# Attention and two MoE blocks on one core: a bound on x from v's sums of squares, new planned durations, filled TensorE gaps, and an order planned anew

## The chip, the cores and the metric

The kernel runs on one core of a Trainium2 chip. The metric is the device time of one execution in microseconds; lower is better. The core has a matrix engine (TensorE, PE in the profile, with its weight loads as PEld), a vector engine (VectorE, DVE), an activation engine (ScalarE, ACT), a general engine (GpSimd, POOL), and a sequencer that issues DMA transfers (SyncE, SP). Each engine works through its own queue in order; they wait for each other by semaphores.

## What is computed

```python
def rmsnorm(x, g):
    rms = np.sqrt(np.mean(x * x, axis=-1, keepdims=True) + 1e-06)
    return x / rms * g
# attention: q, k, v of 4 batches x 12 heads x 448 rows x 64
q_n, k_n = (rmsnorm(q, g_q), rmsnorm(k, g_k))
scores = np.matmul(q_n, k_n.transpose(0, 1, 3, 2)) / np.sqrt(64)
attn = softmax(scores)                       # max taken off, exp, divided by the sum
x = np.matmul(attn, v)                       # -> 1792 tokens x 768
# first block, w_in 768 x 2048, w_out 2048 x 768
h = x @ w_in;  g = h * sigmoid(1.702 * h);  x = g @ w_out
# second block, same sizes
h = x @ w_in2; g = h * np.clip(h + 3, 0, 6) / 6;  out = g @ w_out2
```

Inputs are float64 for the weights (read as 64-bit words and decoded on the chip) and float32 else.

## The kernel before

**Numbers as pairs of halves.** Every float32 operand of a large product is scaled by a power of two and split in two float16 parts, high and low; a product is three float16 matmuls (high x high, low x high, high x low). The scales come from sums of squares: a matmul with a matrix of ones adds them up over the partitions (`total`, L445), and DVE takes the square root's exponent (`root_exponent`, L460 and L463). The high part is a scaled copy on ACT, POOL or DVE (`scaled`: L480, L486, L483), the low part a subtraction on DVE (L495) or, in another form, on POOL or DVE (L510, L511).

**Stages.** For each of the four batches: load q, k and v (L969, L923); norm them (squares L972 or L985, sums L975, k times the gains L978, root L1004 to L1019, times the root L1029, high parts L1035, low parts L1047 and L1050); transpose by DMA; scores on PE (L1204, L1207), maxima on DVE (L1212), exponentials on ACT (L1217); the product with v (batch 0 in fp32: transposes on PE L1266 and products L1132; other batches in halves, L1165); x as halves (L1298 high on ACT, L1303 low on DVE); in-projection on PE (L1411) with a gate on ACT (L1456) and a product on DVE (L1460); out-projection on PE (L1479). The weights of the first block are decoded meanwhile, piece by piece (L618 or L623 the sign, L629, L604 to L614, L635). The attention of batch b + 1 runs beside the projections of batch b. The second block comes last (L1655 and L1770 on PE), by a scheme with fewer products whose operands are sums and differences of blocks (L716, L730).

**The bound on x.** After x's high part is made, `xsquare` (L1309) squares it on ACT and sums it; when all six head pairs are there, DVE takes the largest sum (L1375), a `total` matmul spreads it, and `root_exponent` gives `xe`. `x_scale` (L1390 on) multiplies it into the scale of the gated values. v has its own sums of squares `vm` (L926, once per head pair, on ACT), their largest is taken (L933), and `ev`, `sv`, `xf` are made of it.

**The order** is not written by hand. The program is first recorded as operations with dependencies (`Plan.op`), each with one or more engines that can do it (`ways`) and a planned duration (`t_pe`, `t_act`, `t_dve`, `t_fast` and so on). `Plan.order` then plays the program through with these durations: at each step it takes the operation that can start first, within a look-ahead, by a rank; where several engines can do an operation it picks the one that ends first with a bias per engine added. `Shared` durations are made longer where POOL and DVE work at the same time (`beside`). `LAG` is the planned time from one engine's end to another's start. The numbers in `CFG` shift ranks and biases; `own` shifts single operations by their place in the program. `keep_busy` puts matmuls without use (`fill`, L1960, 512 columns) into PE's queue where the plan sees a gap longer than `late` + `idle` and a PSUM bank is free:

```python
t1 -= CFG['late'] + CFG['idle']
if t1 <= t0 or not t0:
    return
...
n, i = int((t1 - t0) / 215.0) + 1, min(free)[1]
```

`late` (789) stays; `idle` is 1000 before. On the chip only the semaphores hold an engine: a planned gap is no wait by itself.

Of the kernel before, what the change touches and what calls it, by code (L numbers as in the profile page):

```python
# [9 lines left out]
F16 = mybir.dt.float16  # L10
# [24 lines left out]
    bias=[2580, 340, 2500, 1380, 5660],  # L35
    pw=[847, 1827, 3991690324, 32301064499],
    pn=[78, 1413, 6578, 11344],
    ps=[1104, 851, 1934, 2727],
# [4 lines left out]
    look=[0, 130, 60, 920, 540],  # L43
    off=[-9158, 408922, -29895, 22854, 24586, 19810, -27690, 67476, -181023, 15083, 120686, -34408, -37087, -37194, -689989, -31399, -23083, -347804, 11747, 208998],
    abias=44617,
    cuts=[],
    bias0=[2000, 440, 370, 120, 3040],
    bias1=[8820, 1540, 3900, 3250, 4520],
    dlook=2054,
    warm=9,  # L50
    late=789,
    idle=1000,
    pu=419,
    pmost=5,
    pv=1315,
    early_k=[0, 0, 0, 0],
    beside=0.9,
    own={
# [17 lines left out]
    [0.0, 0.0, 0.0, 0.0, 0.0],  # L76
# [3 lines left out]
def t_pe(n):  # L80
    return 0.445 * n
# [26 lines left out]
def t_dve_bits(n):  # L108
    return Shared(1.04 * n + 150)
# [6 lines left out]
def t_pool2(n):  # L116
    return Shared(1.5 * n + 380)
# [213 lines left out]
def attention_moe_moe_kernel(ctx, tc, q, k, v, g_q, g_k, w_in1, w_out1, w_in2, w_out2, out):  # L331
# [71 lines left out]
    bot_t, bot_ring = row(p_m, 19712, 1, [128, S], F16)  # L403
# [35 lines left out]
    def total(m, n, deps, slack=0.0):  # L439

        lease = Lease(mm_ring)
        t = lambda: mm_t[lease.slot][:, :n]

        def emit():
            nc.tensor.matmul(t(), lhsT=one.to_broadcast([128, 128]), rhs=m, start=True, stop=True)  # L445

        o = op((PE, 420, emit), deps, takes=lease)
        o.slack = slack
        return o, t, lease
# [112 lines left out]
    class Weight:  # L562
# [22 lines left out]
        def decoded(self, src, raw, cl):  # L585
# [60 lines left out]
            if self.wide:  # L646
                x = op([(POOL, t_pool(n), sign), (DVE, t_fast(n), sign_dve)], [o], takes=cl)
                x = op((DVE, t_fast(n), decode_a), [x])
                o = op([(POOL, t_pool(n), rebias_pool), (ACT, t_act(n), rebias_act), (DVE, t_fast(n), rebias_dve)], [x])
# [5 lines left out]
        def add(self, i, m, after):  # L655
# [3 lines left out]
            for j in range(i, i + m):  # L659
# [9 lines left out]
                squares.append(op((ACT, t_act(n, 1) + 45, square), [o] + after))  # L669
# [13 lines left out]
            o = op((DVE, 480 if self.inward else 550, scale), [o], gives=wl)  # L683
# [53 lines left out]
    class Units:  # L737
# [8 lines left out]
        def add(self, q, after, free):  # L746
# [7 lines left out]
            for j in range(2):  # L754
# [55 lines left out]
                if self.wide:  # L810
                    x = op([(POOL, t_pool(n), sign), (DVE, t_fast(n), sign_dve)], [o] + ends[:1], takes=None if j else lease)
                    x = op((DVE, t_fast(n), decode_a), [x])
                    o = op([(POOL, t_pool(n), rebias_pool), (ACT, t_act(n), rebias_act), (DVE, t_fast(n), rebias_dve)], [x])
# [4 lines left out]
                squares.append(op((ACT, t_act(n, 1) + 45, square), [o], gives=raw))  # L818
# [82 lines left out]
    class Batch:  # L901


        def __init__(self, b):
# [7 lines left out]
            self.xm, self.xe, self.t1 = small(NP), small(), small()  # L912
            self.c1, self.kg, self.x2m, self.x2e = small(KF), small(KF), small(KD), small()

    def add_values(bt, after):
# [16 lines left out]
        def largest():  # L932
            nc.vector.tensor_reduce(out=m, in_=bt.vm, axis=AX.X, op=ALU.max)  # L933
# [10 lines left out]
    def add_norm(bt, after):  # L944
# [136 lines left out]
        for grp in groups:  # L1081
# [3 lines left out]
                (DVE, 2300, lambda n=grp[0], m=m: root(n, m)), sum((p[1] for p in parts), [])  # L1085
# [84 lines left out]
    def add_units(bt, exp_after, arena_after, x_after):  # L1170
        b = bt.b
        bt.xlow, bt.pvs, xmax = [], [], []
# [6 lines left out]
        for n in range(NP):  # L1179
# [9 lines left out]
            ready = [None, None]  # L1189
            for grp in groups:  # L1190
# [45 lines left out]
                o = op((DVE, t_dve(m * S) + 60, maxes), [o])  # L1236
# [6 lines left out]
                o = op((DVE, 140, inv_z), es)  # L1243
# [15 lines left out]
                else:  # L1259
                    for i, tile_ in enumerate(grp):  # L1260
# [12 lines left out]
                        x = op((PE, 875, flip), [x], takes=tl, gives=dl)  # L1273
# [5 lines left out]
                for h, tiles_ in ((0, range(4)), (1, range(3, 7))):  # L1279
                    if ready[h] is None and all(turns[i] is not None for i in tiles_):  # L1280
                        pieces = [(128 * j, 0, 128, slots[4 * h + j]) for j in range(3)]
                        pieces.append((384, 64 * h, 64, slots[3]))
                        deps = [turns[i] for i in tiles_]
                        ready[h] = (join(pieces), deps) if b else add_head0(bt, n, h, pieces, deps)

            bl = Lease(bot_ring)
            bot = lambda bl=bl: bot_t[bl.slot]
# [29 lines left out]
            if b:  # L1317
# [12 lines left out]
                o = op((PE, 12 * t_pe(S) + 700, both_heads), deps[0] + deps[1] + vdone, takes=ml, gives=vl)  # L1330
# [3 lines left out]
                sq = op((ACT, t_act(S, 1), xsquare), [h], takes=bl, gives=bl)  # L1334
                xmax.append(sq)
                if early:
# [10 lines left out]
                    early.left = 2  # L1347
# [660 lines left out]
```

## Time and profile before

| | us |
|---|---|
| median of 3 runs | 1143.24 |
| lowest and highest | 1141.17, 1145.11 |
| the profiled execution | 1143.13 |
| its span, first to last instruction | 1141.3 |
| PE busy in the span | 1066.2 |
| DVE, ACT, POOL busy | 820.3, 721.0, 366.7 |

The profile names each instruction by engine, line, operation and tiles. Matmuls overlap in the array, so a busy PE is not a PE at its peak; the granted clock stands beside. A wait is put down to the instruction whose semaphore came last.

### The profile page before, as it was taken

The numbers are of one execution on the slowest core, as the hardware profiler recorded it, in microseconds if no ns is written. First come the engines' busy times: TensorE is split into PE (matmuls) and PEld (weight loads), VectorE is DVE, ScalarE is ACT, GpSimd is POOL, SyncE is SP. The second block draws the span as 40 slices with busy tenths as digits, with TensorE's granted clock in tenths as the row PEclk, the third lists the DMA queues.
The fourth block names the chain that finished last, engine by engine and source line by source line (L and its number), as shares of the span: only waits on it lengthen the run. The fifth ranks groups of instructions, "written<-read, shape, count | busy, mean of one in ns | idle before, by whom it ended". The sixth has DMA issues, their size and how long they took to land. (4 is left out here: it accounts for less than half of the span.)

```text
span 1141.3 us, 18028 instructions
## 1 busy us (share of the span) xinstructions
PE 1066.2 (93%) x6571; PEld 588.8 (52%) x6571; DVE 820.3 (72%) x1445; ACT 721.0 (63%) x1503; POOL 366.7 (32%) x337
## 2 busy tenths in 40 slices
PE   3888955999999999989999999999999999999998
PEld 1666522554554555545545555555555555555555
DVE  7998889988699764797765877694577456935342
ACT  5999868999868996578885646474565133512210
POOL 6764565443156101350001346452122103200000
PEclk9999985999999999999999999999999999999999
DMA  8876578999886997579895427733451151123034
GB/s 253 184 201 187 182 214 195 210 185 226 241 221 189 173 180 155 173 201 163 170 192 139 138 66 235 262 107 134 142 194 56 56 170 53 59 68 102 1 90 104
DMA packets 236712, 178.88 MB, mean 157 GB/s; under 512 B 194896, under 2 KB 220496, under 8 KB 235088
## 3 DMA queue, kind: packets, MB, share of 16 engines
q1 hardware_dynamic: 236624, 177.74, 59.6%
q8 instruction: 51, 0.84, 0.3%
q14 instruction: 37, 0.30, 0.1%
HBM read 97.88 MB, written 34.41 MB: 116 GB/s over the span
## 5 line engine op out<-in xcount | busy, mean ns | idle before, releaser
L1411 PE MATMUL mm<-xt,wa 128*128 128x448 f16 x1152 | 229.3, 357 | 6.0 <-DVE st L1460 5.9
L1479 PE MATMUL mm<-gt,wb 128*128 128x448 f16 x1152 | 228.2, 354 | 0.7 <-DVE wb L495 0.5
L1655 PE MATMUL mm<-wa,xt 128*128 128x448 f16 x972 | 189.0, 352 | 0.9 <-ACT wb L1677 0.9
L1770 PEld LDWEIGHTS <-gt 128*128 128x128 f16 x1344 | 131.5, 98 | 90.6 <-issue 2.7
L1411 PEld LDWEIGHTS <-wa 128*128 128x128 f16 x1152 | 113.9, 100 | 113.7 <-issue 14.2
L1479 PEld LDWEIGHTS <-wb 128*128 128x128 f16 x1152 | 112.3, 99 | 105.0 <-issue 3.1
L1655 PEld LDWEIGHTS <-xt 128*128 128x128 f16 x1008 | 98.5, 98 | 91.2 <-issue 1.4
L1217 ACT ACTIVATE p<-s,smalls 128x448 f32<-128x448 f32 x168 | 120.7, 720 | 7.1 <-DVE p L495 3.0
L1770 PE MATMUL s<-gt 128*128 128x384 f16 x576 | 99.3, 326 | 0.0
L1770 PE MATMUL s<-p,gt 128*128 128x384 f16 x516 | 96.2, 326 | 1.1 <-DVE wb L1809 0.5
L1212 DVE TENSOR_REDUCE smalls<-s 128x2 f32<-128x896 f32 (+1 forms) x96 | 91.5, 964 | 4.8 <-PE s L1207 4.7
L495 DVE SCALAR_TENSOR_TENSOR p<-p,smalls 128x448 f16<-128x448 f32 x108 | 78.1, 752 | 21.5 <-ACT p L480 21.2
L1204 PE MATMUL s<-gt 128*128 128x448 f16 (+1 forms) x192 | 62.6, 372 | 31.1 <-ACT p L1217 29.2
L1809 DVE SCALAR_TENSOR_TENSOR wb<-s,smalls,wb 128x384 f32<-128x384 f32 x69 | 39.7, 611 | 70.8 <-PE s L1770 70.7
L480 ACT ACTIVATE p<-p,smalls 128x448 f16<-128x448 f32 (+2 forms) x120 | 75.9, 667 | 11.1 <-DMA xt<-p 7.5
L1207 PE MATMUL s<-gt 128*128 128x448 f16 (+1 forms) x192 | 62.4, 368 | 0.0
L495 DVE SCALAR_TENSOR_TENSOR gt<-st,smalls,gt 128x448 f16<-128x448 f32 x64 | 52.5, 830 | 6.1 <-ACT gt L480 4.9
L1677 ACT ACTIVATE wb<-mm 128x448 f32<-128x448 f32 x21 | 11.3, 540 | 66.2 <-PE mm L1655 66.2
L480 ACT ACTIVATE gt<-st,smalls 128x448 f16<-128x448 f32 x49 | 32.1, 661 | 29.5 <-DVE st L1460 26.3
L1266 PE MATMUL mm<-gt,p 128*128 128x128 f32 x336 | 44.2, 280 | 6.2 <-DVE xt L1277 1.9
L510 POOL TENSOR_TENSOR p<-p 128x448 f16<-128x448 f32 x17 | 20.1, 1184 | 86.8 <-ACT p L480 70.9
L1165 PE MATMUL mm<-xt,gt 128*64 128x64 f16 (+3 forms) x858 | 47.3, 256 | 0.5 <-DMA xt<-p 0.4
(213 smaller groups left out, 1796.2 us busy)
## 6 DMA issues: line engine op xcount, KB each, us to landing
wr<-in_moe_w_in_dram SPq DMA_DIRECT2D x32, 768.0 KB, 4.9
wa<-park_x SPq DMA_DIRECT2D x21, 672.0 KB, 4.1
wr<-in_moe_w_out_dram SPq DMA_DIRECT2D x12, 1024.0 KB, 6.1
wr<-in_moe_w_out_dram SPq DMA_DIRECT2D x16, 768.0 KB, 4.6
qkd<-xt SPq DMA_DIRECT2D x18, 672.0 KB, 4.8
p<-in_v_dram SPq DMA_DIRECT2D x42, 224.0 KB, 4.1
x2d<-st SPq DMA_DIRECT2D x24, 224.0 KB, 3.0
park_x<-wa SPq DMA_DIRECT2D x2, 2688.0 KB, 13.2
```

Of the source, the lines that this page charges most:

```text
L480: nc.scalar.activation(out=dst(), in_=src(), func=AF.Copy, scale=s)
L495: nc.vector.scalar_tensor_tensor(out=dst(), in0=src(), scalar=s, in1=high(), op0=ALU.mult, op1=ALU.subtract)
L1165: nc.tensor.matmul(mm_t[ml.slot][64 * h:64 * h + 64, c:c + m * w], lhsT=vhl[:, 2 * (i % 4) + i // 4, part], rhs=pt[:, s:s + w, i, q0:q0 + ...
L1204: nc.tensor.matmul(o, lhsT=x[:, 64 * t:64 * t + m], rhs=x[:, 448:896], start=True, stop=False)
L1207: nc.tensor.matmul(o, lhsT=x[:, 64 * t:64 * t + m], rhs=x[:, 896:1344], start=False, stop=True)
L1212: nc.vector.tensor_reduce(out=nb, in_=s_t[sl.slot][:, :m, :S], axis=AX.X, op=ALU.max)
L1217: nc.scalar.activation(out=p(i), in_=s_t[sl.slot][:, i, :S], func=AF.Exp, bias=nb[:, i:i + 1], scale=alpha, accum_out=z[:, i:i + 1],)
L1266: nc.tensor.matmul(mm_t[tl.slot][:, 128 * j:128 * j + 128], lhsT=p(i)[:, c:c + 128], rhs=diag(), start=True, stop=True,)
L1411: nc.tensor.matmul(mm_t[ml.slot][:, :n], lhsT=w.inw(we, kc, f), rhs=x[:, xe, kc, :n], start=(kc == k0 and i == 0), stop=(kc == k1 - 1 and ...
L1479: nc.tensor.matmul(mm_t[ml.slot][:, :S], lhsT=W2.outw(we, fc, d * 128, 128), rhs=gv[:, ge_, fc, :], start=(fc == g.part.start and i == 0), ...
L1655: nc.tensor.matmul(self.bank(k), lhsT=w[:, we, fa, kc], rhs=xs[:, fb, xe, kc], start=first and kc == 0 and j == 0, stop=kc == 2 and j == 2 ...
L1770: nc.tensor.matmul(mm_t[banks[h].slot][:, :half], lhsT=g[:, ge, f, tb * 128:tb * 128 + 128], rhs=w4_t[part % 2][:, f, we, h * half:h * hal ...
```

## The change

1. *The bound on x.* `xsquare`, its buffer, the largest, the `total` matmul and the root for x are taken out. v's sums are now added over the six head pairs instead of their largest being taken, and x is bounded by that: the scale of the gated values uses `ev` and a constant.
2. *Planned durations* of most operations are set anew, `beside` goes from 0.9 to 1.15, and the planned time from a DMA's end to every engine from 0 to 300 ns.
3. *Fills.* `idle` goes from 1000 to 0.
4. *Order.* All of `CFG` that steers the planner is new, `own` entirely.

The diff, cut to its core:

```diff
-    idle=1000,
+    idle=0,
-    beside=0.9,
+    beside=1.15,
     own={
-        1: 18285, 2: 13033, 4: 14353, 7: 16590, 17: 60615, 21: 15124, 23: 56483, 26: 34835, 28: 63794, 29: 27563,
...
+        176: 15568.0, 200: 14590.0, 201: 2188290.0, 414: -9016.0, 418: 4574.0, 607: 1737030.0, 661: 1734682.0,
...
-    [0.0, 0.0, 0.0, 0.0, 0.0],
+    [300.0, 300.0, 300.0, 300.0, 300.0],
...
 def t_pe(n):
-    return 0.445 * n
+    return 0.4225 * n
 def t_fast(n):
-    return Shared(0.72 * n + 80)
+    return Shared(0.57 * n + 75)
 def t_dve_two(n):
-    return Shared(1.04 * n + 150)
+    return Shared(1.04 * n + 80)
 def t_dve_rest(n):
-    return Shared(1.04 * n + 205)
+    return Shared(1.04 * n + 135)
 def t_pool2(n):
-    return Shared(1.5 * n + 380)
+    return Shared(1.5 * n + 260)
...
-        (ACT, t_act(S, 3) + 200 * (i == 0) + 160 * (i == m - 1), lambda i=i, f=exps: f(i)),
+        (ACT, t_act(S, 3) - 35 + 325 * (i == 0) + 235 * (i == m - 1), lambda i=i, f=exps: f(i)),
...
         def largest():
-            nc.vector.tensor_reduce(out=m, in_=bt.vm, axis=AX.X, op=ALU.max)
+            nc.vector.tensor_reduce(out=m, in_=bt.vm, axis=AX.X, op=ALU.add)
...
-            def xsquare(n=n, high=high, bot=bot):
-                nc.scalar.activation(
-                    out=bot(), in_=high(), func=AF.Square, scale=2.0 ** -7, accum_out=bt.xm[:, n:n + 1]
-                )
...
-                sq = op((ACT, t_act(S, 1), xsquare), [h], takes=bl, gives=bl)
-                xmax.append(sq)
...
-        o = op((DVE, 200, largest), xmax + [bt.vscale])
-        o, whole, wl = total(m, 1, [o], 200.0)
-        xe = op((DVE, 330, lambda: root_exponent(bt.xe, whole())), [o], gives=wl)
...
-                times(g.t, emax, bt.ev, 2.0 ** -17)
+                times(g.t, emax, bt.ev, 2.0 ** -11)
...
-                times(g.t, g.t, bt.xe, 1.0)
...
-            bt.xscale.append(op((DVE, 870, x_scale), [xe, x]))
+            bt.xscale.append(op((DVE, 870, x_scale), [x]))
```

**What moves in the queues.** In all, fills go from 36 to 174; POOL's products, subtractions and scalings from 319 to 170, and most of what POOL loses stands on DVE. The two places shown next lie behind batch 0's last fp32 product. In the changed file the lines are: fill L1942, in-projection L1393, `total` L448, root times L1032 (L1029 before), gains L981 (L978), low parts L1050 and L1053 (L1047, L1050), low part by subtraction L513 on POOL and L514 on DVE (L510, L511), scaled copies L489 on POOL (L486).

PE's queue behind the last fp32 product of batch 0, before: three fills, then the in-projection (tiles wa and xt), 54 matmuls of it in a row behind the `total`:

```order
L1960 LDWEIGHTS ident_70
L1960 MATMUL mm_73<-ident_70 128x512
L1411 LDWEIGHTS wa
L1411 MATMUL mm_71<-xt,wa 128x448
L1411 LDWEIGHTS wa
L1411 MATMUL mm_71<-xt,wa 128x448
L1411 LDWEIGHTS wa
L1411 MATMUL mm_71<-xt,wa 128x448
L445 MATMUL mm_73<-smalls 128x1
L1411 LDWEIGHTS wa
L1411 MATMUL mm_72<-xt,wa 128x448
```

The same place now: eight fills, 21 matmuls of the in-projection, and then this; the pair of the last two rows of it stands 82 times, ahead of the in-projection's next matmul:

```order
L1393 LDWEIGHTS wa
L1393 MATMUL mm_71<-xt,wa 128x448
L1942 LDWEIGHTS ident_70
L1942 MATMUL mm_73<-ident_70 128x512
L1942 LDWEIGHTS ident_70
L1942 MATMUL mm_73<-ident_70 128x512
...
L448 MATMUL mm_73<-smalls 128x4
L1942 LDWEIGHTS ident_70
L1942 MATMUL mm_74<-ident_70 128x512
```

So a group of 88 fills (6 and 82, around a `total` of the weights) parts the second from the third block of the in-projection; it stood in one run before.

POOL's queue, norms of batch 1 (tile xt) behind the same place, before:

```order
L978 TENSOR_TENSOR xt<-xt,gp 128x448 x2
L1029 TENSOR_TENSOR xt<-xt,smalls 128x448 x2
L1050 TENSOR_TENSOR xt<-xt 128x7x64
L1047 TENSOR_TENSOR xt<-xt 128x7x64
L486 TENSOR_SCALAR gt<-st,smalls 128x448
L978 TENSOR_TENSOR xt<-xt,gp 128x448 x2
L618 TENSOR_SCALAR wr<-wr 128x1024
L1029 TENSOR_TENSOR xt<-xt,smalls 128x448 x2
L1047 TENSOR_TENSOR xt<-xt 128x7x64 x2
```

And now, with weight pieces (tiles wa, wb and wr) between:

```order
L621 TENSOR_SCALAR wr<-wr 128x1024
L1032 TENSOR_TENSOR xt<-xt,smalls 128x448
L489 TENSOR_SCALAR wa<-wb,smalls 128x6x128
L489 TENSOR_SCALAR wa<-wb 128x6x128
L513 TENSOR_TENSOR wa<-wb,wa 128x6x128
L981 TENSOR_TENSOR xt<-xt,gp 128x448
L1032 TENSOR_TENSOR xt<-xt,smalls 128x448
L489 TENSOR_SCALAR gt<-st,smalls 128x448 x2
```

POOL keeps one gain and one root product per pair of head pairs and none of the low parts.

DVE's queue, the same norms, before:

```order
L1019 SCALAR_TENSOR_TENSOR smalls<-smalls 128x28
L495 SCALAR_TENSOR_TENSOR gt<-p,smalls,gt 128x7x64
L1029 TENSOR_TENSOR xt<-xt,smalls 128x448 x2
L495 SCALAR_TENSOR_TENSOR gt<-p,smalls,gt 128x7x64
L1047 TENSOR_TENSOR xt<-xt 128x7x64
L1050 TENSOR_TENSOR xt<-xt 128x7x64
```

And now:

```order
L1022 SCALAR_TENSOR_TENSOR smalls<-smalls 128x28
L463 TENSOR_SCALAR smalls<-mm_73 128x4
L466 TENSOR_SCALAR smalls<-smalls 128x4
L472 TENSOR_SCALAR smalls<-smalls 128x4
L1032 TENSOR_TENSOR xt<-xt,smalls 128x448 x3
L626 TENSOR_SCALAR wr<-wr 128x1024
L1050 TENSOR_TENSOR xt<-xt 128x7x64
L1053 TENSOR_TENSOR xt<-xt 128x7x64 x2
L1050 TENSOR_TENSOR xt<-xt 128x7x64
```

DVE has three of the four root products and all four low parts, where it had two and two; it does sign extractions (L626) too.

## Rows read from the trace of the kernel before

**Rows 1.** The page's busy line, and slices of 1/40 span (digits are tenths).

```profile
PE 1066.2 (93%) x6571; PEld 588.8 (52%) x6571; DVE 820.3 (72%) x1445; ACT 721.0 (63%) x1503; POOL 366.7 (32%) x337
...
PE   3888955999999999989999999999999999999998
...
DVE  7998889988699764797765877694577456935342
ACT  5999868999868996578885646474565133512210
...
PEclk9999985999999999999999999999999999999999
```

**Rows 2.** PE's waits: engine line <- releaser: us in total, times, longest.

```profile
PE s L1204 <- ACT p L1217: 29.2, 26, 4.8
PE mm L1095 <- POOL gt L1050: 15.5, 1, 15.5
```

**Rows 3.** Windows (us: length, busy by engine, clock, DMA share, GB/s).

```profile
core 0: us, PE busy (x) PEld busy (x) DVE busy (x) ACT busy (x) POOL busy (x), PEclk, DMA share, GB/s
0.00:126.70 126.70, 96.71 (x671) 64.92 (x671) 111.81 (x214) 108.59 (x270) 80.02 (x94) 0.99 0.76 204
126.70:163.40 36.70, 31.56 (x171) 15.71 (x170) 32.37 (x66) 25.43 (x40) 22.47 (x18) 0.95 0.69 199
163.40:190.40 27.00, 7.27 (x23) 2.65 (x22) 25.80 (x48) 20.88 (x48) 14.90 (x12) 0.56 0.86 231
190.40:314.00 123.60, 118.56 (x825) 63.71 (x824) 103.53 (x194) 112.87 (x254) 45.67 (x39) 0.99 0.91 207
314.00:720.00 406.00, 398.15 (x2504) 208.75 (x2504) 301.86 (x541) 297.15 (x658) 124.14 (x111) 0.99 0.73 175
720.00:1141.30 421.30, 413.95 (x2384) 233.09 (x2382) 244.94 (x386) 156.03 (x235) 79.46 (x65) 1.00 0.32 102
```

**Rows 4.** PE in order of time: start, us, instruction, [idle before <- releaser].

```profile
149.75 0.53 PE L1411 MATMUL mm<-xt,wa 128*128 128x448 f16 x1 [4.96 <-DVE st L1460]
...
172.32 0.53 PE L1204 MATMUL s<-gt 128*128 128x448 f16 x1 [3.32 <-ACT p L1217]
...
179.48 0.53 PE L1204 MATMUL s<-gt 128*128 128x448 f16 x1 [4.76 <-ACT p L1217]
...
314.15 8.10 PE L1411 MATMUL mm<-xt,wa 128*128 128x448 f16 x42
```

**Rows 5.** x's squares and maximum by line: ns min/median/max, first and last start.

```profile
L1309 ACT ACTIVATE p<-xt x18: 558/576/577, 54.9 to 611.8; 128x448 f16<-128x448 f16 x18
L1309 ACT ACTIVATION_READ_ACCUMULATOR p<-xt x18: 185/186/191, 55.4 to 612.3; 128x1 f32 x18
...
L1375 DVE TENSOR_REDUCE smalls<-smalls x4: 149/160/160, 133.8 to 612.5; 128x1 f32<-128x6 f32 x4
...
  PEld mm L445: 0.6, 1
```

**Rows 6.** PE in order of time, a group of fills.

```profile
723.36 1.02 PE L1960 MATMUL mm<-ident 128*128 128x512 bf16 x4
724.23 0.28 PE L445 MATMUL mm<-smalls 128*128 128x1 f32 x2
```

**Rows 7.** By line: products and subtractions of 448 columns on DVE and POOL.

```profile
L1029 POOL TENSOR_TENSOR xt<-xt,smalls x21: 934/939/1375, 142.9 to 500.7; 128x448 f32<-128x448 f32 x21
L1029 DVE TENSOR_TENSOR xt<-xt,smalls x15: 612/1354/1452, 144.3 to 501.1; 128x448 f32<-128x448 f32 x15
...
L1050 DVE TENSOR_TENSOR xt<-xt x11: 609/1449/1455, 147.5 to 503.8; 128x448 f16<-128x448 f32 x11
```

**Rows 8.** By line: decoding, scaled copies and low parts on DVE.

```profile
L629 DVE TENSOR_SCALAR wb<-wr x16: 588/609/1367, 12.2 to 115.8; 128x768 uint16<-128x768 uint16 x16
...
L635 DVE SCALAR_TENSOR_TENSOR wb<-wr,wb x16: 933/958/1823, 19.5 to 118.1; 128x768 int32<-128x768 int32 x16
...
L495 DVE SCALAR_TENSOR_TENSOR p<-p,smalls x108: 658/680/1524, 176.7 to 602.7; 128x448 f16<-128x448 f32 x108
...
L495 DVE SCALAR_TENSOR_TENSOR wa<-wb,smalls,wa x14: 995/1006/1965, 50.1 to 130.8; 128x768 f16<-128x768 f32 x14
...
L483 DVE TENSOR_SCALAR gt<-gt,smalls x7: 286/382/940, 36.3 to 124.4; 128x128 f32<-128x128 f32 x7
L483 DVE TENSOR_SCALAR gt<-wb x1: 600/600/600, 14.5 to 14.5; 128x448 f16<-128x448 f32 x1
```

**Rows 9.** PE's waits between 314 and 720 us, the longest sum.

```profile
PE s L1204 <- ACT p L1217: 6.0, 6, 2.8
```

More of the change, by code (lines that the diff above doesn't have):

```diff
@@ L648, in decoded @@
                 x = op((DVE, t_fast(n), decode_a), [x])
-                o = op([(POOL, t_pool(n), rebias_pool), (ACT, t_act(n), rebias_act), (DVE, t_fast(n), rebias_dve)], [x])
+                o = op([(POOL, t_pool(n), rebias_pool), (ACT, t_act(n) + 75, rebias_act), (DVE, t_fast(n), rebias_dve)], [x])
                 o = op((DVE, t_dve_bits(n), decode_b), [o], **done)
@@ L667, in square @@
                     )
-                squares.append(op((ACT, t_act(n, 1) + 45, square), [o] + after))
+                squares.append(op((ACT, t_act(n, 1), square), [o] + after))
                 leases.append(cl)
@@ L812, in add @@
                     x = op((DVE, t_fast(n), decode_a), [x])
-                    o = op([(POOL, t_pool(n), rebias_pool), (ACT, t_act(n), rebias_act), (DVE, t_fast(n), rebias_dve)], [x])
+                    o = op([(POOL, t_pool(n), rebias_pool), (ACT, t_act(n) + 75, rebias_act), (DVE, t_fast(n), rebias_dve)], [x])
                     o = op((DVE, t_dve_bits(n), decode_b), [o])
@@ L817, in add @@
                 ends.append(o)
-                squares.append(op((ACT, t_act(n, 1) + 45, square), [o], gives=raw))
+                squares.append(op((ACT, t_act(n, 1), square), [o], gives=raw))
             def scale(whole):
@@ L1084, in add_norm @@
             rooted = op(
-                (DVE, 2300, lambda n=grp[0], m=m: root(n, m)), sum((p[1] for p in parts), [])
+                (DVE, 2450, lambda n=grp[0], m=m: root(n, m)), sum((p[1] for p in parts), [])
             )
@@ L1188, in add_units @@
                     bt.qkt[n][h].left += 1
-            ready = [None, None]
+            ready, pieces_ = [None, None], []
             for grp in groups:
@@ L1235, in add_units @@
                 bt.scores.append(o)
-                o = op((DVE, t_dve(m * S) + 60, maxes), [o])
+                o = op((DVE, t_dve(m * S), maxes), [o])
                 es = []
@@ L1328, in both_heads @@
                                         product(ml, runs[h][r], i, h, j)
-                o = op((PE, 12 * t_pe(S) + 700, both_heads), deps[0] + deps[1] + vdone, takes=ml, gives=vl)
+                o = op((PE, 2260 + (900 if sum(map(len, runs)) > 4 else 0), both_heads), deps[0] + deps[1] + vdone, takes=ml, gives=vl)
                 pv = [o, o]
@@ L1345, in get @@
                         )
-                    early.left = 2
-                    sq.also.append(early)
                     x = sp(128 * 1792, put, [x], gives=early)
@@ L1360, in both @@
                                 product_(ml, i, j)
-                o = op((PE, 2400, both), deps[0] + deps[1], takes=ml, gives=vls[0])
+                o = op((PE, 3640 + 142 * (8 * sum(len(join(x)) for x in pieces_) - 32), both), deps[0] + deps[1], takes=ml, gives=vls[0])
                 o.also = [vls[1]]
@@ L1366, in add_units @@
                 bt.xlow.append(op((DVE, t_dve(S) + 30, bind(xlow, ml, slice(0, 128))), [x], gives=ml))
-                xmax.append(op((ACT, t_act(S, 1), xsquare), [x], takes=bl, gives=bl))
             for i in range(7):
@@ L1370, in add_units @@
             bt.pvs += pv
-        m = bt.t1
-        def largest():
-            nc.vector.tensor_reduce(out=m, in_=bt.xm, axis=AX.X, op=ALU.max)
-        o = op((DVE, 200, largest), xmax + [bt.vscale])
-        o, whole, wl = total(m, 1, [o], 200.0)
-        xe = op((DVE, 330, lambda: root_exponent(bt.xe, whole())), [o], gives=wl)
         bt.inscale, bt.xscale = [], []
@@ L1446, in add_in @@
                 m = lambda f=f: half(f)
-            o = op((ACT, t_act(n, 2) - 50, lambda f=f, t=t, m=m: gate(f, t(), m())), [o, ready[group(f)]], takes=pl)
+            o = op((ACT, t_act(n, 2) - 110, lambda f=f, t=t, m=m: gate(f, t(), m())), [o, ready[group(f)]], takes=pl)
             o = op((DVE, t_dve(n), lambda t=t, m=m: product(t(), m())), [o], gives=None if early else ml)
@@ L1488, in add_out1 @@
                         deps += W2.done[2 * d:2 * d + 2]
-                    last[0] = op((PE, 3 * t_pe(S) + 8, emit), deps, takes=None if fc > g.part.start else ml)
+                    last[0] = op((PE, 3 * t_pe(S), emit), deps, takes=None if fc > g.part.start else ml)
                 def scale(d=d, g=g):
```

44 lines of the change are left out of this document (21 added, 23 removed), and 20 rows, old and new, of the table own.

## The prediction

> **What bounds the kernel now.** I read the page's busy line and slices first: PE is busy for 93% of the span, and from the eighth slice on nearly always, so what remains to be won or lost is PE's idle time of some 75 us, and it lies in the first fifth, where DVE and ACT show nines while PE shows eights, fives and sixes and its clock falls [rows 1]. Next the list of PE's waits: the largest sums are scores that wait for an exponential on ACT (29.2 us in 26 waits) and the first matmul of all (15.5 us) [rows 2]. Then the windows, cut at places in the program. Up to 126.7 us (the start of batch 0's last fp32 attention product) PE works 96.7 us. From 163.4 to 190.4 it works only 7.27 of 27.0 us at a mean granted clock of 0.56, so mostly at 1.2 GHz instead of 2.4, while DVE is busy for 25.80 us [rows 3]. The rows of PE there are scores of batch 1, held 3 to 5 us each by exponentials, after a wait of 4.96 us for a free PSUM bank [rows 4]. ACT is no more loaded in that stretch (20.88 us) than elsewhere; what its exponentials wait for is DVE: maxima, weight decoding and the norms of the next batch share its queue. So the early stage is bound by DVE, and by how its order fits PE's; from 314.1 us (the first in-projection matmul of batch 1) PE is the bound: 398.15 of 406.00 us, then 413.95 of 421.30 us [rows 3, 4].
>
> **The change, part by part.** The sum is made against the profiled execution, 1143.13 us with a span of 1141.3, so 1.8 us lie around the span; the median of the runs is 1143.24. Code lines are those of before.
>
> *The bound on x.* Out go 24 squares on ACT, each 0.57 us and 0.19 us for its sum [rows 5], 18 us in all, and per batch a maximum, two passes of a small fp32 matmul, and two or three small DVE steps of 0.15 us. ACT is busy for 63% [rows 1], so most of the 18 us hide nothing and free nothing. On PE's path lay only the four small matmuls that stood in its queue until x's last square was summed: 0.6 us is what the rows show of that, once. I take 1 us, between 0 and 2.4 (four such). That the scales come earlier frees the in-projection's result buffers earlier; this is in the stage below.
>
> *The order up to 126.7 us.* Ahead of that matmul stand 212 instructions on DVE before, 199 now. Three weight pieces are decoded later: three L629 (0.61 us), three L635 (0.96), four L495 (1.0), that is 8.7 us less; six scalings L483 by 0.38 less, 2.3 us; eight sign extractions more, priced as their neighbour L629, 4.9 us, and two gains by 0.61 [rows 7, 8]. Net -5 us. DVE is busy for 111.81 of the 126.70 us [rows 3], so PE follows in part: I take -3. The ends are -6, and +2 because POOL now squares two tiles ahead of the first gain, and the first matmul waits for POOL's chain [rows 2].
>
> *The order from 126.7 to 314.1 us.* This term decides. Between the two places DVE had 306 instructions and gets 349; POOL had 60 and gets 37. Of the 43 more on DVE, 25 are subtractions and products of 448 columns that POOL did (ten L511, four each of L978, L1047, L1029, three L1050). DVE takes 0.61 us for one alone and 1.35 to 1.45 us (the medians) where POOL works beside it [rows 7]; 11 such stood on DVE here before. If POOL is out of the way, 36 x 0.61 - 11 x 1.4 = +6.6 us; if not, 25 x 1.4 = +35. POOL loses 23 of its 60, so I take the first. The three weight pieces that were put off add 8.7 us, six scalings L483 of 448 columns 3.6 (at 0.60), five sign extractions 3.4. Together +22. Other DVE instructions that POOL used to slow get shorter; from nothing up to 23 x 0.94 us of POOL's time [rows 7], less the 8.8 already counted, so 0 to 13. I take 5, since the median of L495, 0.68 us, is near its minimum [rows 8]. DVE's busy time here then goes from 161.7 us (the three windows) to 179 us. What time that fills depends on DVE's share: 0.88, 0.956 and 0.84 in the three windows [rows 3]. At 0.956 it is 187 us, just the 187.4 of before; at the mean 0.863 it is 207.
>
> PE sets the other end. It was busy for 157.4 us here, of which the 7.27 us at clock 0.56 would be 4 at full clock, so 154; and the new plan puts 122 fill matmuls in this stretch, 0.22 us each (four stand between 723.36 us and the next matmul at 724.23) [rows 6], 27 us that PE must run whether its inputs are there or not. 154 + 27 = 181 us, against 187.4. The fills stand where the new plan itself expects PE to wait, 88 of them in one place, right where the stall of before begins. So the stall is not planned away, it is filled: the clock stays up, some 3 us. I take 187 us, no change, near PE's end because DVE held 0.956 in just the window that counts; the ends are -6 and +20.
>
> The Trainium skill bears on the 23 instructions taken from POOL: "SBUF — State Buffer", section "SBUF: two separate sides", says that DVE instructions with two SBUF inputs and GpSimd hold one pair of ports in turn, and that the loser blocks for the whole instruction. L1029's 1.35 us against 0.61 [rows 7] agrees; by that rule in full the relief would be the 13 us, and the sum 8 us lower: the second rival.
>
> *After 314.1 us.* DVE gets heavier here too, but has room: 301.86 of 406 us and 244.94 of 421.3 [rows 3]. Up to 720 us PE waits 6.0 us for exponentials [rows 9]; the plan's longer exponentials and transfers should place those scores better, so half of it goes: -3, ends 0 and -6. In the last stage 21 fills stand where 6 stood; 15 x 0.22 = 3.3 us, partly in a real wait: +2, ends 0 and +3.3.
>
> The prices given to the planner move nothing by themselves. Sum: -1 - 3 + 0 - 3 + 2 = -5 us, 1143.1 - 5 = **1138 us**.
>
> **The rivals.** *DVE becomes the limit (slower).* For: +22 us of DVE work, in a stretch where it was at 0.86, and a prefix that grows on a queue which PE, ACT and the transposes all wait for; what is lost there is kept, since PE has no slack after. Against: 0.956 in the stall. At 0.863 the stretch is 207 us: -1 - 3 + 20 - 3 + 2 = +15, 1158 us. It decides from a share below about 0.93 (179/0.93 = 192, +5 us, which eats the rest).
>
> *POOL's absence pays in full (much faster).* DVE's work is then 171 us and PE's 181 us stand alone: -6 there, -6 before, -8 from waits and x's matmuls, no cost from the last fills: -20, 1123 us. For: the medians beside POOL are more than twice the minima [rows 7]. Against: most of DVE's time in this stretch is L495, maxima and PSUM reads, which were not twice as long.
>
> *The fills hold PE (the change doesn't do what it says).* A fill runs though the work behind it is ready; if DVE is ahead of the plan, half of the 137 added fills cost time: 137 x 0.22 / 2 = +15, less the 5 won: 1153 us. Against: the stall of before was 27 us long in this place without being planned.
>
> **How the numbers follow.** Forecast (1131 to 1146) 0.40; DVE the limit 0.28; POOL's absence in full 0.22; fills 0.10. About 0.3%, 3.4 us, is what a measurement of this kernel can tell from no change. Of the forecast's case 0.24 lies below 1139.8 and 0.14 within 0.3%; with the rivals faster is 0.46, same 0.18, slower 0.36. Both signs hold much, so the range reaches from the fast rival to the slow one: 1120 to 1160 us; the forecast's own is 1131 to 1146.
>
> **What would show it.** Right: the first in-projection matmul of batch 1 between 305 and 316 us; clock near 1.0 from 160 to 195 us; DVE above 0.93 from the last fp32 product to there; the median of L1029 on DVE near 0.61 us. Wrong: that matmul past 320 us with DVE below 0.9 (first rival), or fills that end while the next matmul's inputs had long been there (third). A gain or loss of over 5 us after 314 us would also make it wrong: there I expect almost none.

## The result, and the profile after

The changed kernel is slower: 1149.45 us against 1143.26 of the kernel before beside it, a ratio of 1.0058 [1.0041, 1.0076]; in a second set 1149.38 against 1140.98, 1.0071 [1.0056, 1.0085]. The forecast was 1138 us. The direction was wrong. The time lies in the stated range, above the forecast and below its two slower rivals (1153 and 1158 us); the range held it by its width. The profiled execution has a span of 1147.5 us, 6.2 more than before.

From the page of the changed kernel: busy time of each engine and slices of 1/40 of the span (digits are tenths).

```profile
PE 1083.8 (94%) x6701; PEld 598.5 (52%) x6701; DVE 849.8 (74%) x1595; ACT 705.0 (61%) x1438; POOL 181.6 (16%) x188
...
PE   3799986799998999999999999989999999999998
...
DVE  6998899999789975698676878694668546936342
ACT  4899777988768896679784645464665132522210
...
PEclk9999998899999999999999999999999999999999
```

Against [rows 1] POOL does half of what it did, DVE 30 us more, and PE's seventh and eighth slices are a six and a seven, where the sixth and seventh were fives. The clock falls less there.

PE's largest waits in the changed kernel (us in total, times, longest):

```profile
PE mm L1098 <- POOL gt L1053: 18.9, 1, 18.9
PE mm L1393 <- DVE st L1442: 13.5, 7, 7.5
PE s L1207 <- ACT p L1220: 12.4, 8, 7.2
```

The waits for exponentials fell from 29.2 us in 26 to 12.4 in 8, and one of 7.2 is more than half of that [rows 2]. In their place stand waits for gate products (L1442; 5.9 us in 3 before) and a wait of the first matmul that is 3.4 us longer.

The windows of the changed kernel, cut at the same matmuls of PE: the start of the last fp32 product of batch 0 (121.6), the first matmul of in-projection block 7 of batch 0, counted from 0 (193.7), and the first in-projection matmul of batch 1 (324.8). The two cuts 10 and 30 us behind block 7 stand where PE has done as many matmuls in both kernels, the fills left out, though not the same ones. Then the kernel before between these places.

```profile
core 0: us, PE busy (x) PEld busy (x) DVE busy (x) ACT busy (x) POOL busy (x), PEclk, DMA share, GB/s
0.00:121.60 121.60, 93.39 (x673) 63.81 (x673) 103.31 (x202) 98.38 (x243) 68.05 (x95) 1.00 0.72 184
121.60:193.70 72.10, 60.01 (x303) 28.09 (x303) 67.55 (x141) 49.90 (x93) 20.58 (x18) 0.95 0.84 230
193.70:203.90 10.20, 10.20 (x57) 5.52 (x56) 10.13 (x19) 10.10 (x22) 3.71 (x3) 1.00 0.85 215
203.90:223.60 19.70, 11.12 (x81) 5.52 (x79) 19.16 (x40) 19.29 (x44) 6.04 (x5) 0.74 1.05 191
223.60:324.80 101.20, 98.59 (x698) 53.87 (x697) 86.01 (x169) 79.05 (x177) 23.95 (x19) 1.00 0.94 212
```

```profile
126.70:190.40 63.70, 38.83 (x192) 18.36 (x192) 58.17 (x113) 46.31 (x88) 37.37 (x30) 0.79 0.76 212
190.40:202.20 11.80, 11.80 (x56) 5.86 (x55) 11.69 (x18) 9.85 (x20) 4.42 (x4) 0.85 0.55 107
202.20:210.60 8.40, 8.40 (x78) 4.70 (x76) 8.40 (x13) 7.62 (x18) 4.01 (x4) 1.00 1.10 265
210.60:314.10 103.50, 98.46 (x697) 53.26 (x696) 83.54 (x165) 95.39 (x218) 37.34 (x33) 1.00 0.93 214
```

The changed kernel is 5.1 us ahead at the first place, 3.3 behind at block 7, and 13 behind at 223.6; from there to batch 1 it gets 2 back. Two stretches lose: the one from the product to block 7 by 8.4 us, the short one by 11.3. In the short one PE does 8.4 us of work in the kernel before while DVE does 13 instructions and ACT 18; now DVE does 40 and ACT 44, they are busy for 19.2 and 19.3 of the 19.7 us, and PE waits for them. The rows of PE there, with the first large wait:

```profile
182.82 2.40 PE L1393 MATMUL mm<-xt,wa 128*128 128x448 f16 x6 [7.53 <-DVE st L1442]
...
218.46 0.53 PE L1207 MATMUL s<-gt 128*128 128x448 f16 x1 [7.24 <-ACT p L1220]
...
219.88 5.47 PE L1393 MATMUL mm<-xt,wa 128*128 128x448 f16 x18 [0.29 <-DVE st L1442]
```

### The profile page after: what moved, and what is told of

Same layout as the page of the kernel before. It is cut to its first block, busy times and chain, and to the rows that moved or that the text cites. A ratio compares the mean times of both kernels' runs of the same rounds, so it can differ in the third digit from the quotient of the medians.

```text
span 1147.5 us, 18089 instructions
## 1 busy us (share of the span) xinstructions
PE 1083.8 (94%) x6701; PEld 598.5 (52%) x6701; DVE 849.8 (74%) x1595; ACT 705.0 (61%) x1438; POOL 181.6 (16%) x188
## 4 chain that ended last, share of the span: by engine, by line
PE 68%; DVE 16%; ACT 4%; DMA 3%; issue 2%; SPq 0%; POOL 0%; DVEq 0%; POOLq 0%; ACTq 0%
PE mm L1461 17%; PE s L1752 15%; PE mm L1637 14%; PE mm L1393 12%; PE mm L1168 3%; PE mm L1752 3%; PE s L1207 2%; DMA wr<-in_moe_w_out_dram 2%; DVE gt L498 1%; PE s L1210 1%; DVE smalls L1215 1%; DVE p L498 1%; PE mm L1269 1%; DVE gt L733 1%; DVE st L1442 1%
## 5 line engine op out<-in xcount | busy, mean ns | idle before, releaser
L1393 PE MATMUL mm<-xt,wa 128*128 128x448 f16 x1152 | 229.7, 356 | 13.5 <-DVE st L1442 13.5
L1461 PE MATMUL mm<-gt,wb 128*128 128x448 f16 x1152 | 225.3, 352 | 0.7 <-DVE gt L498 0.7
L1637 PE MATMUL mm<-wa,xt 128*128 128x448 f16 x1008 | 196.0, 352 | 0.6 <-DVE st L1652 0.6
L1393 PEld LDWEIGHTS <-wa 128*128 128x128 f16 x1152 | 113.0, 99 | 120.4 <-issue 20.2
L1752 PE MATMUL s<-p,gt 128*128 128x384 f16 x528 | 100.6, 326 | 2.6 <-ACT gt L483 1.4
L498 DVE SCALAR_TENSOR_TENSOR p<-p,smalls 128x448 f16<-128x448 f32 x108 | 75.7, 723 | 13.2 <-ACT p L483 12.8
L1207 PE MATMUL s<-gt 128*128 128x448 f16 (+1 forms) x192 | 60.9, 363 | 15.2 <-ACT p L1220 12.4
L1210 PE MATMUL s<-gt 128*128 128x448 f16 (+1 forms) x192 | 60.1, 356 | 0.0
L1438 ACT ACTIVATE st<-mm,smalls 128x448 f32<-128x448 f32 x64 | 39.2, 626 | 20.9 <-PE mm L1393 18.6
L498 DVE SCALAR_TENSOR_TENSOR gt<-st,smalls,gt 128x448 f16<-128x448 f32 x64 | 46.5, 736 | 3.0 <-ACT gt L483 2.9
L1652 DVE TENSOR_TENSOR wb<-mm,wb 128x448 f32<-128x448 f32 x24 | 14.9, 622 | 42.6 <-PE mm L1637 40.0
```

The costliest lines, as they stand in the source:

```text
L498: nc.vector.scalar_tensor_tensor(out=dst(), in0=src(), scalar=s, in1=high(), op0=ALU.mult, op1=ALU.subtract)
L1207: nc.tensor.matmul(o, lhsT=x[:, 64 * t:64 * t + m], rhs=x[:, 448:896], start=True, stop=False)
L1210: nc.tensor.matmul(o, lhsT=x[:, 64 * t:64 * t + m], rhs=x[:, 896:1344], start=False, stop=True)
L1393: nc.tensor.matmul(mm_t[ml.slot][:, :n], lhsT=w.inw(we, kc, f), rhs=x[:, xe, kc, :n], start=(kc == k0 and i == 0), stop=(kc == k1 - 1 and ...
L1461: nc.tensor.matmul(mm_t[ml.slot][:, :S], lhsT=W2.outw(we, fc, d * 128, 128), rhs=gv[:, ge_, fc, :], start=(fc == g.part.start and i == 0), ...
L1637: nc.tensor.matmul(self.bank(k), lhsT=w[:, we, fa, kc], rhs=xs[:, fb, xe, kc], start=first and kc == 0 and j == 0, stop=kc == 2 and j == 2 ...
```

## The experiments

Most kernels here replay an order from a table: for each operation its place, its engine and its buffer, all as the planner of one of the two kernels chose them. Where two orders are joined, the second gives what the first has not yet done. The diffs show the rule by which the table was made. All have the new bound on x. Each set has its own runs of the kernel before (1140.8 to 1141.9 us).

```diff
-        self.order()
+        replay(self, ORDER)
         for o in self.done:
             o.way[2]()
```

**Are the fills to blame?** Without the 122 of the middle:

```diff
-ORDER = AFTER
+ORDER = [x for i, x in enumerate(AFTER) if not (fill(x) and PV < i < IN1)]
```

> The changed kernel, same order on every engine, without the 122 fill matmuls between the last fp32 product of batch 0 and the first in-projection matmul of batch 1; all other fills stay. If DVE is what is late there (its busy share was 0.94 and 0.97 in the two windows from 119 to 225 us), the fills only stood in waits: that in-projection matmul stays at 325 us within 3, the time at 1149.5 within 2, or up to 3 us above it if the clock falls where the fills stood. If the fills hold PE, half of 122 x 0.22 us is won: 312 us and 1136.

Measured: 1150.6 us, 1.0089 [1.0075, 1.0104]; block 7 at 194.7, the in-projection matmul at 324.9. This ratio is from another chip than the first one of the changed kernel, so the worth of the fills was settled side by side, without any of them and with the order of all else unchanged:

```diff
-    idle=0,
+    idle=1e9,
```

> The changed kernel as it is, beside the next run on the same chip. If the fills are worth little, its ratio to the kernel before is that of the run without the 122 fills, 1.008 to 1.009; if they kept 3 to 4 us, it stays at 1.005 to 1.006.

> The changed kernel without any of its 174 fills, order unchanged. If fills hold PE anywhere, it is faster than the changed kernel beside it, by up to 174 x 0.22 = 38 us if no cover is there. If they stand in waits only and keep the clock up, it is slower, by 2 to 6 us (in the kernel before, the clock fell to 0.56 over 27 us of stall). If neither, the same within 2 us.

Measured: 1149.38 us with, 1149.19 without any fill (1.0071 [1.0056, 1.0085] and 1.0077 [1.0061, 1.0093]): the same. The first ratio lies between the two that I had named. The window from the last fp32 product to block 7, without fills:

```profile
121.80:194.90 73.10, 42.49 (x186) 18.89 (x186) 69.94 (x143) 50.68 (x96) 21.46 (x18) 0.77 0.79 232
```

PE's busy time drops from 60.01 to 42.49 us, the clock from 0.95 to 0.77, and the stretch is 1.0 us longer, which the kernel's time does not show. The third rival falls, and so does the gain from a clock that is kept up: neither shows in the time. The section "Why this matters for your kernels" of the Trainium skill's page "TensorE: Matmul & The Clock Gate" advises to keep TensorE busy for its full rate. In the rows above it has the full rate where it is always busy, but for the 0.85 right behind the stall of before (190.4 to 202.2 us); where it waits for DVE, the higher clock left the end of the wait where it was.

**The bound on x alone**, in the order of before.

```diff
-                sq = op((ACT, t_act(S, 1), xsquare), [h], takes=bl, gives=bl)
-                xmax.append(sq)
...
-        xe = op((DVE, 330, lambda: root_exponent(bt.xe, whole())), [o], gives=wl)
```

> The kernel before, its order, engines and buffers kept for every operation, with only the bound on x changed (the 24 squares, the maxima, the small totals and their exponents are gone). By my term 1 us is won, between 0 and 2.4: 1142.2 (1140.8 to 1143.3). If ACT's 18 us count where scores wait for exponentials, more: up to 5 us, 1138. If it costs something (a bound that comes in another place of DVE's queue), above 1143.3.

Measured: 1139.12 against 1141.18 us, 0.9984 [0.9971, 0.9997]: 2.1 us less, inside the term's bounds, though the interval reaches from 0.3 to 3.3 us.

**Which part of the order loses?** The two orders joined at the last fp32 product (PV) or at batch 1's first in-projection matmul (IN1), both ways:

```diff
+e3: ORDER = AFTER[:PV + 1] + rest(BEFORE)
+e5: ORDER = BEFORE[:PV + 1] + rest(AFTER)
+e4: ORDER = BEFORE[:IN1 + 1] + rest(AFTER)
```

> The changed kernel's order up to and with the last fp32 product of batch 0, and behind it what is left in the order of the kernel before (its bound on x is the new one). The changed kernel came to that place 6 us earlier than the one before. If the order behind it is what loses (by 17 us up to the first in-projection matmul of batch 1), the lead is kept: 1143.3 - 6 - 1 = 1136, and that matmul comes at 308. If the early lead was borrowed (DVE work that was put off and has to be done in any order behind it, some 13 us of it), the stall of 27 us of before grows by about as much: 1143 to 1149.

Measured: 1145.44 us, 1.0041 [1.0028, 1.0054]; block 7 at 198.9 us, the in-projection matmul at 319.9. The lead of 5 us at the product became a lag of 8 at block 7: a debt, work put off that has to be done all the same.

> The order of the kernel before up to and with the last fp32 product of batch 0 (new bound on x), and behind it what is left in the changed kernel's order: the other half of the exchange. From there to the first in-projection matmul of batch 1 the changed kernel lost 17 us. With the changed order only ahead of that place, 14 us were lost behind it. If that debt (DVE work put off ahead of the place) and the work taken from POOL behind it add, what is left here is the second alone: +3 to +8 us at that matmul, 317 to 322 us, and 1143 to 1147 against 1141.2 of the kernel before in the first set. If the changed order behind the place loses whatever stands ahead of it: 331 us, and 1153. If the debt was all: 314 us, 1140.

Measured: 1152.33 us, 1.0089 [1.0070, 1.0108]; block 7 at 195.8, block 10 at 221.9, the in-projection matmul at 326.4. So the changed order behind the product loses all of it, without the debt too.

> The order of the kernel before up to the first in-projection matmul of batch 1 (new bound on x), and behind it what is left in the changed kernel's order. Behind that place the changed kernel gave 9 us back by 480 us and lost 4 in the last stage. If its order there is better by itself: 1143.3 - 1 - 9 + 4 = 1137. If only its lateness was absorbed there (PE came later, so nothing had to be waited for), the 9 us are not to be had: 1143 to 1147.

Measured: 1140.33 us, 0.9994 [0.9983, 1.0005]: 1 us behind the bound on x alone, no gain in all, so nearer to the second theory. In its trace, against the kernel before where PE has done as much, it lost 8 us from the seam, where the orders are joined, to 350 us, was some 6 ahead at 600, and lost 4 in the last stage. Without the fills there:

> The run with the order of before up to the first in-projection matmul of batch 1 and the changed order behind it, here without the 21 fills of the last stage. In that run 4 us were lost where these fills stand (6.6 us ahead of the kernel before at 666 us, 2.4 ahead at 762). If the fills hold PE: 21 x 0.215 = 4.5 us less, 1136 against 1140.3 (1141.2 before). If they only stood in a wait of the same length: no change, 1140.

Measured: 1141.06 us, 0.9994 [0.9980, 1.0008]; in the trace nearly 4 us were lost there all the same. Not the fills.

**Is it the work taken from POOL?** In the changed order back to POOL (e6), and in the order of before over to DVE (e7):

```diff
+e6: ORDER = [(k, POOL if k in MOVED else e, s) for k, e, s in AFTER]
+e7: ORDER = [(k, DVE if k in MOVED else e, s) for k, e, s in BEFORE]
```

> The changed kernel with its own order, and the 38 operations that it took from POOL to DVE between the last fp32 product of batch 0 and the first in-projection matmul of batch 1 issued on POOL again, each at its old place in the program. They are 38 x 0.6 = 23 us of DVE's time. If DVE's amount of work sets that stretch, it gets shorter by 5 to 12 us: the in-projection matmul at 313 to 320 us and the time 0 to 5 us above the kernel before. If POOL's work slows DVE by as much as it relieves it (an instruction of 448 columns took 1.35 to 1.45 us beside POOL in the kernel before), or the chain behind these results gets longer by POOL's slower turn, nothing changes or it gets slower: 325 us and later, 7 us or more above the kernel before.

> The mirror: the order of the kernel before with the new bound on x (as in the run with that bound alone, 2 us under the kernel before), and 34 of the same operations in the same stretch issued on DVE instead of POOL, in place. If DVE's work sets the stretch: +5 to +12 us against that run, that is 3 to 10 us above the kernel before. If POOL's absence pays in full (my second rival: 23 x 0.94 us relieved), it is faster than the run with the bound alone: 3 us or more under the kernel before.

Measured: 1151.93 us with POOL again, 1.0091 [1.0072, 1.0109], the in-projection matmul at 328.1; 1139.21 us with the work on DVE in the old order, 0.9979 [0.9966, 0.9993], like the bound on x alone. Neither came out as DVE's amount of work or POOL's absence in full would have it; the move is not the cause. In e6 DVE's share of the stretch from the product to batch 1 fell to 0.85 (175.9 of 206.1 us), and the stretch got no shorter. The windows from the last fp32 product to block 7 and on to batch 1, of the bound alone and of e7:

```profile
128.20:192.40 64.20, 39.06 (x189) 18.29 (x190) 56.52 (x109) 45.56 (x86) 36.41 (x30) 0.78 0.78 211
192.40:313.40 121.00, 117.08 (x825) 63.56 (x824) 105.39 (x194) 109.66 (x242) 46.01 (x39) 0.99 0.92 213
```

```profile
127.20:191.20 64.00, 39.48 (x190) 18.34 (x190) 58.83 (x124) 45.72 (x86) 18.42 (x15) 0.79 0.74 211
191.20:315.10 123.90, 119.27 (x826) 63.97 (x825) 110.19 (x214) 109.79 (x242) 21.98 (x20) 0.97 0.91 208
```

DVE got 35 instructions more, and its busy time grew by 7.1 us (161.9 to 169.0), 0.2 us each, while POOL's fell by 42. The rest came back from instructions that POOL no longer slowed, such as L1032 on DVE, in the bound alone and then in e7:

```profile
L1032 DVE TENSOR_TENSOR xt<-xt,smalls x5: 618/1352/1356, 147.9 to 179.6; 128x448 f32<-128x448 f32 x5
...
L1032 DVE TENSOR_TENSOR xt<-xt,smalls x9: 609/612/1350, 146.8 to 179.8; 128x448 f32<-128x448 f32 x9
```

The Trainium skill's page "SBUF — State Buffer", section "SBUF: two separate sides", states that DVE instructions with two SBUF inputs and GpSimd share a pair of ports that one of them holds for its whole instruction while the other is blocked; the medians, 1.35 us and 0.61, agree with it. PE's time did not follow: its stretch took 187.9 us instead of 185.2.

**Does the amount of DVE's work count at all?** The bound alone, without the normalisation of batch 1's q and k:

```diff
             def norm(eng, i):
+                if b == 1:
+                    return
```

> The run with the bound on x alone, without the 12 multiplications that normalise q and k of batch 1 (the scores of that batch come from unnormalised q and k, so this part of the computation is left out). 5 of them stand on DVE ahead of in-projection block 7 of batch 0 (6.0 us there), the rest on POOL or behind. In every order so far that block began at 190 to 199 us with DVE busy for 170 to 174 us by then. If the amount of DVE's work sets when the stall ahead of block 7 ends, it begins 6 us or more earlier, 186 us or less against 192.4, and the time falls by about as much. If the order and the chain through ACT and the transposes set it, 2 us or less.

Measured: 1134.8 us, 0.9942 [0.9921, 0.9964]. Up to block 7, the bound alone and this kernel:

```profile
0.00:192.40 192.40, 138.38 (x860) 85.03 (x861) 167.92 (x322) 152.25 (x345) 115.05 (x123) 0.90 0.76 205
...
0.00:187.00 187.00, 136.46 (x860) 83.53 (x861) 162.37 (x317) 151.46 (x345) 107.75 (x116) 0.92 0.78 211
```

DVE has 5.6 us less to do and block 7 begins 5.4 us sooner; about all of it is kept to the end. In this order, then, less work on DVE pays nearly one for one up to block 7. Some of it may be the chain behind the left-out step, 7 of whose 12 instructions stood on POOL; that was not tried apart. The changed kernel had 170.9 us of DVE's work done by block 7, before 170.0 [rows 3 and the windows above]: what was put off ahead of the product had to be done by then all the same. But the amount alone does not fix the place. Up to block 7, in e5 and e3:

```profile
0.00:195.80 195.80, 157.71 (x972) 94.59 (x973) 168.64 (x339) 149.85 (x341) 97.63 (x109) 0.97 0.74 199
...
0.00:198.90 198.90, 135.84 (x864) 83.06 (x865) 170.99 (x322) 151.42 (x340) 108.61 (x128) 0.89 0.72 198
```

For 169 to 171 us of DVE's work the block began at 190.4 (before), 193.7 (changed), 195.8 (e5) and 198.9 us (e3): the order also sets how long DVE idles ahead of it, 20 to 28 us, and which of its waits make the difference stays open.

**The short stretch at 204 us.** First one block moved ahead; from the order of ACT:

```
 L483 ACTIVATE gt<-st,smalls 128x448
+L1438 ACTIVATE st<-mm_73,smalls 128x448
 L483 ACTIVATE p<-p,smalls 128x448 x3
```

> The changed kernel with one thing moved: in-projection block 10 of batch 0 stands on PE ahead of three groups of scores of batch 1 instead of behind them, and the gates and products of blocks 7 and 8, which free its PSUM bank, stand on ACT and DVE where these blocks have just ended. Nothing is added or taken away, no fill either. In the changed kernel block 10 began at 219.9 us, 11 us later than PE's work before it allows, behind a wait of 7.2 us for an exponential. If this order is what loses the time, 5 to 10 us come back: the first in-projection matmul of batch 1 at 315 to 320 us and the time 0 to 2 us above the kernel before. If ACT and DVE are simply full there (they had no idle time from 203 to 219 us), the wait moves to another matmul, and the time stays 6 to 7 us above the kernel before.

Measured: 1150.53 us, 1.0083 [1.0062, 1.0104]; the in-projection matmul at 325.9. Block 10 came at 212.2 us, 7.7 sooner, and behind it:

```profile
222.68 0.53 PE L1207 MATMUL s<-gt 128*128 128x448 f16 x1 [5.12 <-ACT p L1220]
...
226.09 4.78 PE L1168 MATMUL mm<-xt,gt 128*64 128x384 f16 x55 [2.29 <-DVE smalls L463]
```

The wait moved on, as the second theory had it: ACT and DVE are full. So the orders were exchanged at the end of block 9 (B9), where both have done nearly the same:

```diff
+e12: ORDER = AFTER[:B9 + 1] + rest(BEFORE)
+e13: ORDER = BEFORE[:B9 + 1] + rest(AFTER)
```

> The changed kernel's order up to the end of in-projection block 9 of batch 0 (206 us there), and behind it what is left in the order of the kernel before. At that place the two kernels are 2 us apart in PE's work and within 1 us in DVE's. If the changed order behind block 9 loses the 11 us (scores of batch 1, whose maxima and exponentials DVE and ACT still have to do, ahead of in-projection blocks that need little of them), they are not lost here: block 10 at 210 us or before, the first in-projection matmul of batch 1 at 314 to 317 us, and the time within 2 us of the kernel before. If the loss was only put off by that place, it comes all the same: 322 us or later, 6 us or more above it.

> The other half: the order of the kernel before up to the end of block 9 of batch 0 (203 us there), and behind it what is left in the changed kernel's order. If the changed order behind block 9 is the cause: block 10 at 214 to 220 us instead of 204, the first in-projection matmul of batch 1 at 322 to 326 us, and the time 5 to 9 us above the kernel before. If it needs what stands ahead of it: 315 us, no more than 2 us above.

Measured: e13 1150.46 us, 1.0090 [1.0073, 1.0106]; block 10 at 220.1, the in-projection matmul at 324.5: with the old order up to block 9 the changed order behind it loses the whole 11 us. Its windows around the place, and the wait:

```profile
191.00:202.20 11.20, 11.20 (x54) 5.54 (x53) 11.09 (x18) 9.32 (x20) 3.90 (x3) 0.86 0.57 113
202.20:223.80 21.60, 11.46 (x81) 5.98 (x79) 18.54 (x41) 19.76 (x47) 2.58 (x2) 0.79 0.96 190
```

```profile
219.11 0.53 PE L1207 MATMUL s<-gt 128*128 128x448 f16 x1 [7.54 <-ACT p L1220]
```

The same number of PE's matmuls behind block 9 in the bound alone:

```profile
203.40:211.80 8.40, 8.40 (x77) 4.72 (x76) 8.40 (x13) 7.63 (x19) 3.95 (x5) 1.00 0.99 251
```

At the end of this stretch e13 has read 3 groups of scores more on DVE than the bound alone, and ACT has done 12.4 us more: 6 exponentials with their sums, and 8 scalings of their results. PE's queue holds the scores of batch 1 ahead of in-projection blocks that need little of either engine. e12: 1146.66 us, 1.0047 [1.0034, 1.0060]; block 10 at 210.4, the in-projection matmul at 320.2. The 7 us wait is gone, but the stretch still loses 4 us, 2.2 of them in a wait for a gate product (L1442); whether the seam or the early debt makes them stays open, and my bound of 2 us above the kernel before was missed:

```profile
206.20:218.60 12.40, 10.22 (x77) 5.16 (x76) 11.07 (x19) 10.33 (x22) 7.28 (x6) 0.86 0.62 140
```

Of the 6.8 us that e12 is late at the in-projection matmul against the bound alone, 3.6 were lost by block 7. So the changed order loses in two places, and its two halves do not simply add (1.0090 and 1.0047, against 1.0058 to 1.0071 for the whole).

**A version that beats both.** The changed order only where it gains, from about 400 us (e11) or 445 us (e14) to the out-projection of batch 2, the order of before around it:

```diff
+ORDER = BEFORE[:CUT + 1]; ORDER += rest(AFTER[:OUT2 + 1]); ORDER += rest(BEFORE)
```

> New bound on x, and three parts: the order of the kernel before up to the last group of scores but a few in batch 1's in-projection (about 391 us), the changed order from there to the out-projection of batch 2 (about 667 us), and the order of before for the rest. In the changed kernel this middle part took 9 us less than before, the stretches on both sides more. If that gain belongs to the order: 1141.2 - 2 - 8 = 1131. If it was only lateness that was absorbed: 1139, as with the bound on x alone.

> As the run of three parts, but the changed order begins later, in the out-projection of batch 1 (about 445 us), at a place where it is ahead of the order of before by 9 DVE operations, a DMA and one operation of PE and behind it by none. In the run of three parts 6 us were lost right behind the first cut and 11 gained after 440 us. If the 6 us were those of the seam, 3 or more of them stay: 1133 or less where the run of three parts had 1137 and the kernel before 1141. If the gain after 440 us needs what the changed order does ahead of it: 1138 to 1140, as with the bound on x alone.

Measured: 1136.81 us, 0.9963 [0.9949, 0.9976], and 1136.39, 0.9962 [0.9949, 0.9975]: 4.5 us under the kernel before, 11 to 12 under the changed one by the ratios. That lies between what the two theories gave. About half of the gain is the bound on x, which had 0.9984 alone; what the order adds, some 2 us, is no larger than the width of these intervals. In e14's trace the lead over before was some 7 us at 603 us and was kept; at the seam some 6 us were lost in both, so the later cut did not help.

## Why the prediction was wrong

**The step that failed** is the order from 126.7 to 314.1 us: "I take 187 us, no change, near PE's end because DVE held 0.956 in just the window that counts". It was 203.2 us (324.8 - 121.6), 15.8 more than before. The terms under it were close: DVE's work 182.9 us instead of 179, PE's 179.9 instead of 181; 35 moved instructions cost 7.1 us net in e7, where 6.6 was reckoned for 25. What failed is to set two sums against each other over 187 us. Inside, the limits change: up to block 7 it is DVE, by its work and by its waits (e9, e5, e3), from 204 us on DVE and ACT together (e13), elsewhere PE. What PE lost in the second it could not win back in the third, though over the whole stretch each engine had room. ACT, which had 177.7 us of work done at 223.6 us where it had 172.4 before, stood in no term of this sum. And a stretch's share of DVE is a result: 0.90 in the changed kernel, 0.85 with 38 operations back on POOL, and the time was no shorter (e6).

**Up to 126.7 us**: -3, ends -6 and +2; it was -5.1. Right in itself, but no gain: DVE's 8.5 us of work that were put off here (103.3 instead of 111.8) had to be done by block 7, which came 3.3 us later than before. The prediction added them to the next stretch and still let PE's end decide there. They are not all of what was lost up to block 7: without them the changed order took 68.4 us from the product to the block (e5), with them 72.1, and before 63.7.

**The bound on x**: -1; 2.1 us less, alone. Within 0 to -2.4.

**After 314.1 us**: -3 and +2; it was -4.5 (822.7 us from batch 1's first in-projection matmul to the end, 827.2 before). The waits of [rows 9] fell from 6.0 us to 0.4, while those for gate products rose from 0.5 to 3.6. Whether the new order makes the gain is not shown here: the old one took as little where it got there late too (823.2 us in e3, 823.3 in e12), and from 820.8 to 826.0 us where it was on time (e7 and the bound alone). The last stage lost 4 us, but not by the fills (e8, e16): the reason given for +2 was wrong, and the cause stays open.

**The fills and the clock**: "some 3 us" for a clock kept up. The granted clock was 0.95 between the product and block 7, where it had been 0.79, and that was worth nothing (e16).

**The rivals.** "DVE becomes the limit" had the sign and the place right: the matmul came past 320 us, and DVE's share was 0.90, under the 0.93 from which it was to decide and at the edge of the "below 0.9" asked for. Its reason, the work taken from POOL, falls (e6, e7), and its 20 us for the stretch were 15.8, which 5.1 us won ahead of it and 4.5 behind it brought down to 6.2 in the span. "POOL's absence pays in full" was right on DVE's time and wrong on the kernel's. "The fills hold PE" falls (e1, e16).

**The signs named**: the median of L1032 on DVE (0.62 us in the changed kernel) was as I wanted it for "right", and the clock of 0.90 from 160 to 195 us partly so; DVE's 0.90 was under the 0.93 wanted, and the matmul at 325 us was the sign for "wrong". The first is no sign of the kernel's time.

## What to carry to other kernels

Compare two orders at places where the limiting engine has done the same work, and read there what each other engine has done by then: a lead of PE with less work done on DVE is a debt, and a row of work that is light on PE and heavy on DVE and ACT, put ahead of the opposite, is paid at once by an engine that later has no slack. To find which part of a new order is good, join it with the old one at such places and run both halves: here it turned a loss of 6 us into a gain of 4.5, of which the bound on x alone makes 2.

## What was not expected of the hardware

Taking 174 fill matmuls out lowered the clock from 0.95 to 0.77 between the last fp32 product and block 7 and left the time the same (1149.38 and 1149.19 us). And 35 instructions of about 0.6 us moved from POOL cost DVE 7.1 us, not 21 (e7).
